# An mLSTM cell feeding a gated MLP: copies and joins of the first cells in another order, and two steps moved in later periods

## The chip, the cores and the metric

The kernel runs on one core of a Trainium2 chip. A core has five engines that run their own queues of instructions in order and wait for each other through semaphores: TensorE (PE, matmuls; its weight loads are shown as PEld), VectorE (DVE), ScalarE (ACT), GpSimd (POOL) and SyncE (SP), which here only issues DMA copies. The metric is the device time of one execution in microseconds, given as the median of several executions.

## The reference, cut to what matters

Two blocks are chained. The first is an mLSTM cell with 4 batch rows, 8 heads, 768 steps and a head size of 40:

```
m_new = max(f + m, i);  f_stab = exp(f + m - m_new);  i_stab = exp(i - m_new)
C = f_stab * C + i_stab * outer(v, k);   n = f_stab * n + i_stab * k
y = sigmoid(o_gate) * (C q) / max(|n . q|, 1)
```

The second takes the 3072 x 320 result x: `h = x @ w_in` (320 x 2048), `g = h * cos(h)`, `out = g @ w_out` (2048 x 320). All is float32.

## The kernel before, in words

The recurrence is worked in 6 chunks of 128 steps. One *cell* n is one chunk of one batch row (8 heads), so there are 24 cells, n = 4 * chunk + row. For a cell the kernel takes the scores k.q (scores, line 443), weighs them with a decay matrix E of 128 x 1024 (weigh, line 453), multiplies by v (values, line 469), divides by the denominator and multiplies by the sigmoid of the output gate (normalize, line 528, giving z), and turns z for the MLP (seam, line 572; seam_out, line 593, copies it to xT). seam also makes the update of the state, pu, which state (line 599) copies or adds. E is a broadcast copy from DRAM (load_E, line 340), from which a per-column value is subtracted (decay_exponents, line 370: VectorE line 372, then GpSimd's select, line 373), and then ScalarE's exp (decay, line 380). The queries and keys are turned by TensorE (turn, line 424; turn_out, line 435, copies them out of PSUM). From cell TURNED = 7 on they are instead loaded in blocks and turned by VectorE (turn_blocks, line 406), and turn_gates (line 414) multiplies the query by its gate and turns the output gates.

The MLP takes a chunk of 4 rows (512 columns) at a time. Up (line 610) multiplies two blocks of 128 rows of w_in with xT (lines 624 and 627, the second for the last 64 rows of w_in, held in w_in_l). h * cos(h) takes four steps a block: near (ScalarE, line 632), rest (VectorE, 635), sin (ScalarE, 640), gate (VectorE, 644). PSUM holds one pair of blocks, so the next Up waits for the gate of the one before. down (line 747) multiplies g with w_out and adds up. From chunk 1 on down_parted (line 686) uses seven products of half width for two of the rows; it needs differences of w_out (differences, line 658) and sums of g (sums, line 675), both made by GpSimd.

The weights come as 64-bit numbers. They are loaded in pieces (weights_in, line 156: two pieces of 512 columns and one for w_in_l; weights_out, line 167), and made into float32 by parts (line 132: two ScalarE steps, lines 138 and 140) and join (line 143: three VectorE steps, lines 144, 146 and 148, and an addition on GpSimd or VectorE, line 149).

The order of the work is written out by hand: no scheduler moves an instruction. first_cells (line 771) works cells 0 to 3 and prepares cell 4, with warm (line 766) putting matmuls without use between. Then both_parts(c, b) (line 907) is a *period*: two Ups of chunk c, with the work of cell 4(c+1)+b between them. The gates of each period stand in VectorE's queue with the joins, the cell's normalization and the turns, so VectorE's order sets when the next Up may start. All copies but four go through SP's queue, in its order; ScalarE loads a table (ACT_TABLE_LOAD) where it goes from one of exp, sigmoid and sin to another.

PSUM tiles come from three pools of rotating buffers: ps_u (2 buffers; its first two tiles are pw and pmu, used by the first cells), ps_a (2) and ps_o (4). psum(n) (line 397) gives the pool of a cell's tiles.

Of the kernel before, what the change touches and what calls it, by code (L numbers as in the profile page):

```python
# [29 lines left out]
def kernel(  # L30
# [22 lines left out]
    B, H, S, D = q.shape  # L53
# [16 lines left out]
    TURNED = 2 * B - 1  # L70
# [269 lines left out]
    def load_E(n):  # L340
        c, b = divmod(n, B)
        E = p4.tile([128, H, C], FP, name="E", tag="E")
        if n not in SPREAD:
            src = M_d[0][ts(b, H)] if c == 0 else M_d[1][ts(b, H), ts(c - 1, C)]
            nc.sync.dma_start(out=E, in_=src.unsqueeze(0).to_broadcast([128, H, C]))
        Es[n] = E
# [225 lines left out]
    def seam(n):  # L572

        pool, tag = psum(n)
        if n < TURNED:

            px = pmu[:, 0:NK + 1] if n < B - 1 else pool.tile([128, NK + 1, C], FP, name="px", tag=tag)
            for i in range(NK + 1):
                nc.tensor.transpose(px[:, i], ys[n][:, ts(i, 128)], ident)
            pxs[n] = px  # L580
        if n < N - B:

            if n < B - 1:
                pu = pw.rearrange("r p t -> r (p t)")[:, 0:HP * D1].rearrange("r (p d) -> r p d", p=HP)
            else:
                pu = pool.tile([128, HP, D1], FP, name="pu", tag=tag)
            for p in range(HP):
                for j in range(2):
                    nc.tensor.matmul(pu[64 * j:64 * j + D, p], kws[n][:, 2 * p + j], vs[n % NB][:, 2 * p + j],  # L589
                                     start=True, stop=True)  # L590
            pus[n] = pu
# [63 lines left out]
    def parted(c):  # L655
        return c > 0
# [114 lines left out]
    def first_cells():  # L771
        nc.vector.memset(nil, 0.0)
        gates_in()
        nc.scalar.copy(out=ident_b, in_=ident)
        load(0, "qk")
        later_gates_in()
        load(1, "qk")
        load(0, "v")
        load_o(0, (0, 1))
        load(2, "qk")  # L780
        load_E(0)
        load_E(1)
        warm(9)
        gates_first()
        later_fills()
        gates_first_out()
        wall_in(0, 0, pmu)
        wall_in(0, 1, psum_o())
        spread(0, 0)
        decay_exponents_half(0, 0)  # L790
        turn(0)
        turn_out(0, False)
        gates_sums()
        spread(0, 1)
        decay_exponents_half(0, 1)
        decay(0)
        weigh_k(0)
        load_E(2)
        load(1, "v")
        load(3, "qk")  # L800
        load_o(0, (2, 3))
        load_E(3)
        load(2, "v")
        load(3, "v")
        pieces.extend(weights_in(0))
        wall_in(1, 0, psum_o())
        wall_in(1, 1, psum_o())
        gates_less_sums()
        spread(1, 0)
        decay_exponents_half(1, 0)  # L810
        scores(0)
        gates_maxima()
        turn(1)
        weigh(0)
        turn_out(1, False)
        sigmoid(0, slice(0, 2))
        spread(1, 1)
        decay_exponents_half(1, 1)
        gates_exponents()
        decay(1)  # L820
        weigh_k(1)
        values(0)
        normalize(0)
        scores(1)
        turn(2)
        turn_out(2, False)
        warm(2)
        seam(0)
        weigh(1)
        seam_out(0)  # L830
        state(0)
        load(B)
        decay_exponents(2)
        decay(2)
        weigh_k(2)
        gates_exp()
        values(1)
        load_E(B)
        outs.append((0, weights_out(0)))
        load_o(1, (0,))  # L840
        load_E(B + 1)
        normalize(1)
        scores(2)
        turn(3)
        sigmoid(0, slice(2, 4))
        seam(1)
        weigh(2)
        decay_exponents(3)
        turn_out(3)
        gates_diagonal()  # L850
        seam_out(1)
        values(2)
        decay(3)
        weigh_k(3)
        state(1)
        normalize(2)
        scores(3)
        pg = gates_turn()
        warm(1)
        seam(2)  # L860
        weigh(3)
        join(*parts(*pieces.pop(0)))
        pieces.extend(weights_in(1))
        load(B + 1)
        outs.extend((p, weights_out(p)) for p in range(1, 3))
        load_o(1, (1, 2, 3))
        seam_out(2)
        second = parts(*pieces.pop(0))
        state(2)
        gates_keep(*pg)  # L870
        values(3)
        normalize(3)
        warm(5)
        seam(3)
        join(*second, nc.vector)
        decay_exponents(B)
        seam_out(3)
        join(*parts(*pieces.pop(0)), nc.vector)
        load_E(B + 2)
        state(3)  # L880

    def cell_after_first():
# [24 lines left out]
    def both_parts(c, b):  # L907

        n = (c + 1) * B + b
        cell = n < N
        begin = c == b == 0
        more = cell and n + 1 < N
        f2 = 2 * b
        up = Up(c, f2, cell_after_first if begin else None)
        if cell:
            scores(n)
            if begin:  # L920
                values_kept(n)

                warm(6, psum_o())
        for e in range(2):
            up.near(e)
        if begin:
            weigh(n)
        for e in range(2):
            up.rest(e)
        if cell and not begin:  # L930
            weigh(n)
        if begin or more and c > 0:
            decay_exponents(n + 1)
        for e in range(2):
            up.sin(e)
            up.gate(e)
        sums(c, f2)
        if n == TURNED:
            turn_gates(n)
        if c == 0 and b == 1:  # L940
            sigmoid(1, slice(1, B))
        if begin:
            sigmoid(1, slice(0, 1))
        if b == B - 1 and c + 2 < NC:
            sigmoid(c + 2)
        h = ()
        if c == 0 and not begin:
            out_join(*out_parts())
        if pieces:
            h = parts(*pieces.pop(0))  # L950
        rest = None
        if b == 0 and c > 0 and parted(c - 1):
            rest = down(c - 1, NF // 2 - 1)
        if begin or more and c > 0:
            decay(n + 1)
        elif more:
            decay_by_bias(n + 1)
        if f2 > 0:
            down(c, f2 - 1)
        elif rest:  # L960
            rest()
        elif c > 0:
            down(c - 1, NF // 2 - 1)
        if cell:
            if n + 2 < N:
                load(n + 2)
            if n < TURNED:
                if not begin:
                    values_kept(n)
                values(n)  # L970
                normalize(n)
            else:
                values_turned(n)
            if h:
                join(*h)
            if TURNED <= n + 2 < N:
                load_G(n + 2)
            if n + 3 < N:
                load_E(n + 3)
            if b == B - 2 and c + 2 < NC:  # L980
                load_o(c + 2)
            if n >= TURNED:
                normalize_turned(n)
            fade(n)
        h = ()
        sin_next()
        if pieces:
            h = parts(*pieces.pop(0))
        up = Up(c, f2 + 1)
        if cell:  # L990
            seam(n)
        for e in range(2):
            up.near(e)
        for e in range(2):
            up.rest(e)
        if cell and n < TURNED:
            seam_out(n)
        if h:
            join(*h)
        if cell:  # L1000
            state(n)
        for e in range(2):
            up.sin(e)
            up.gate(e)
        sums(c, f2 + 1)
        if more:
            weigh_k(n + 1)
        if c == 0 and b == B - 1 or c == 1 and b < B - 1:
            two_differences(c * (2 * b + 2))
        if pieces:  # L1010
            join(*parts(*pieces.pop(0)))
        down(c, f2)
        if pieces:
            join(*parts(*pieces.pop(0)))
        if c == 0:
            if b + 2 < B:
                pieces.extend(weights_in(b + 2))
            h = out_parts()
        if more and n + 1 < TURNED:
            turn(n + 1)  # L1020
            turn_out(n + 1, c > 0)
        elif more:
            turn_blocks(n + 1)
            if n + 1 > TURNED:
                turn_gates(n + 1)
        if c == 0:
            out_join(*h)

    pieces, outs = [], []
    with tc.manual_schedule():  # L1030
# [35 lines left out]
```

## Time and profile before

| What | us |
|---|---|
| Median of 3 executions (lowest, highest) | 537.99 (536.78, 539.98) |
| The profiled execution's own time | 537.05 |
| Its span, first to last instruction | 535.3 |
| TensorE busy | 522.5 |
| VectorE busy | 368.9 |
| ScalarE busy | 260.5 |
| GpSimd busy | 167.8 |
| First Up begins | 35.42 |
| Last matmul ends | 531.8 |

The span is what the engines' instructions take from first to last; the execution's own time is longer by what lies around it. Busy time counts instructions, not queues that wait. Matmul times overlap, so a busy TensorE is not one at its peak. The timeline names a group of like instructions by start, duration, engine, line, operation and tiles; in brackets stands how long the engine was idle before it, and what ended that. The waits list an engine's line, whom it waited for, the total, the number of times and the longest. The chain follows the work that ended last back to what released each step.

In 40 slices of the span, the 16 DMA engines are 90% busy or more in the first eight slices (to 107 us) and less later.

### The profile page before, as it was taken

Reading aid. Unit: us, or ns where it says so; the run is one execution under the profiler, and the core shown is the slowest. Engines: PE = TensorE matmul, PEld = TensorE weight load, DVE = VectorE, ACT = ScalarE, POOL = GpSimd, SP = SyncE. Lnnn points to the kernel's source line nnn. Section 1 sums busy time; section 2 is a strip of 40 time slices with the busy share of each in tenths; the row PEclk is TensorE's granted clock in tenths of the full one; section 3 lists DMA queues with packets and bytes.
Section 4 is the critical chain, followed back from the end, with each engine's and each line's share of the span. In section 5 each row is a group of like instructions: output and inputs, shape, how many; then the busy total and the mean of one; then the engine's idle time right before and its main releaser. Section 6 shows DMA issues by size and latency. Waiting matters only on the chain.

```text
span 535.3 us, 10028 instructions
## 1 busy us (share of the span) xinstructions
PE 522.5 (98%) x3663; PEld 329.9 (62%) x3663; DVE 368.9 (69%) x734; ACT 260.5 (49%) x413; POOL 167.8 (31%) x305
## 2 busy tenths in 40 slices
PE   9888999999999999999999999999999999999997
PEld 6755666655565665566666656656756756656555
DVE  6778778898777687777767777767776765422323
ACT  4868696774633544543436525427335322332312
POOL 7512433525263453223222322422212211212121
PEclk9999999999999999999999999999999999999999
DMA  9999999942265742166735076535075000010001
GB/s 136 216 219 236 218 229 226 206 110 64 83 130 128 159 100 74 62 130 141 154 75 113 13 174 140 140 81 120 7 181 106 11 15 11 8 47 2 0 0 50
DMA packets 134857, 57.76 MB, mean 108 GB/s; under 512 B 70248, under 2 KB 130872, under 8 KB 134808
## 3 DMA queue, kind: packets, MB, share of 16 engines
q1 hardware_dynamic: 134664, 56.93, 47.7%
q8 instruction: 29, 0.48, 0.4%
q0 software_dynamic: 96, 0.18, 0.2%
q14 instruction: 20, 0.16, 0.1%
q10 hardware_dynamic: 48, 0.02, 0.0%
HBM read 50.76 MB, written 6.34 MB: 107 GB/s over the span
## 4 chain that ended last, share of the span: by engine, by line
PE 82%; SPq 5%; DMA 4%; DVE 4%; ACT 2%; issue 1%; POOL 1%; DVEq 0%; POOLq 0%; ACTq 0%
PE po L700 32%; PE pup L624 28%; PE pup L627 9%; PE po L757 3%; PE hp L493 3%; PE ps L450 3%; SPq L329 2%; PE hp L487 2%; DMA bits<-in_moe_w_in_dram 1%; DMA E<-M_d 1%; SPq L129 1%; PE pu L589 1%; DMA qs<-in_q_dram 1%; DVE wt L148 1%; SPq L300 1%
## 5 line engine op out<-in xcount | busy, mean ns | idle before, releaser
L624 PE MATMUL pup<-xT,w_in_sb 128*128 128x512 f32 x384 | 175.1, 598 | 0.7 <-DVE g L644 0.3
L632 ACT ACTIVATE n<-pup 128x512 int32<-128x512 f32 x96 | 52.0, 593 | 212.5 <-PE pup L627 212.5
L635 DVE SCALAR_TENSOR_TENSOR n<-pup,n 128x512 f32<-128x512 f32 x96 | 61.9, 686 | 119.9 <-ACT n L632 119.9
L700 PE MATMUL po<-w_out_sb,g 128*128 128x320 f32 (+1 forms) x480 | 118.6, 396 | 0.0
L624 PEld LDWEIGHTS pup<-xT,w_in_sb 128*128 128x128 f32 x384 | 69.7, 190 | 73.2 <-issue 63.4
L700 PEld LDWEIGHTS po<-w_out_sb,g 128*128 128x128 f32 x480 | 83.5, 190 | 36.7 <-issue 9.1
L683 POOL TENSOR_TENSOR sg<-g 128x128 f32<-128x128 f32 x80 | 36.6, 458 | 193.0 <-DVE g L644 191.6
L640 ACT ACTIVATE n<-n 128x512 f32<-128x512 f32 x96 | 58.9, 630 | 12.4 <-DVE n L635 12.4
L644 DVE SCALAR_TENSOR_TENSOR g<-pup,n 128x512 f32<-128x512 f32 x96 | 61.7, 685 | 2.5 <-ACT n L640 1.2
L627 PE MATMUL pup<-xT,w_in_l 64*128 64x512 f32 x192 | 54.2, 641 | 2.0 <-DVE w_in_l L149 2.0
L373 POOL TENSOR_SCALAR_AFFINE_SELECT E<-E 128x1024 f32<-128x1024 f32 x19 | 20.8, 1094 | 101.5 <-DVE E L372 80.4
L700 PE MATMUL po<-T,sg 128*128 128x160 f32 x240 | 39.4, 300 | 0.0
L757 PE MATMUL po<-w_out_sb,g 128*128 128x320 f32 x128 | 36.6, 439 | 1.7 <-POOL w_out_sb L149 1.7
L627 PEld LDWEIGHTS pup<-xT,w_in_l 64*128 64x128 f32 x192 | 14.4, 184 | 38.5 <-issue 35.6
L700 PEld LDWEIGHTS po<-T,sg 128*128 128x128 f32 x240 | 34.8, 190 | 0.2
L411 DVE STREAM_TRANSPOSE t<-qs 128x512 f32<-128x512 f32 x34 | 34.7, 1098 | 0.0
L450 PEld LDWEIGHTS ps<-t,t 40*128 40x128 f32 (+1 forms) x384 | 25.1, 188 | 9.7 <-issue 9.4
L456 DVE TENSOR_TENSOR E<-ps,E 128x512 f32<-128x512 f32 x48 | 30.7, 681 | 0.4 <-PE ps L450 0.4
L381 ACT ACTIVATE E<-E 128x1024 f32<-128x1024 f32 x21 | 22.2, 1057 | 17.5 <-POOL E L373 16.2
L757 PEld LDWEIGHTS po<-w_out_sb,g 128*128 128x128 f32 x128 | 23.7, 190 | 11.4 <-POOL w_out_sb L149 2.1
L450 PE MATMUL ps<-t,t 40*128 40x128 f32 (+1 forms) x384 | 25.8, 274 | 0.0
L372 DVE TENSOR_TENSOR E<-E,tab 128x1024 f32<-128x1024 f32 x19 | 23.1, 1217 | 3.4 <-DMA E<-M_d 3.4
(152 smaller groups left out, 634.3 us busy)
## 6 DMA issues: line engine op xcount, KB each, us to landing
E<-M_d SPq DMA_DIRECT2D x22, 512.0 KB
bits<-in_moe_w_in_dram SPq DMA_DIRECT2D x40, 128.0 KB
bits<-in_moe_w_out_dram SPq DMA_DIRECT2D x8, 640.0 KB
room<-G_d SPq DMA_DIRECT2D x34, 128.0 KB
ks<-in_k_dram SPq DMA_DIRECT2D x24, 160.0 KB
vs<-in_v_dram SPq DMA_DIRECT2D x24, 160.0 KB
o<-in_o_gate_dram SPq DMA_DIRECT2D x68, 40.0 KB
qs<-in_q_dram SPq DMA_DIRECT2D x34, 80.0 KB
```

The lines of the kernel that those rows point to most:

```text
L411: nc.vector.transpose(out=dst.rearrange("r p (t x) -> r p x t", x=T4), in_=src.rearrange("r p (x d) -> r p x d", x=T4)[:, :, :, 0:32])
L450: nc.tensor.matmul(ps[j][:, p], kT[r, p], qT[r, p], start=True, stop=True)
L456: nc.vector.tensor_tensor(out=w, in0=pss[n][j], in1=w, op=OP.mult)
L624: nc.tensor.matmul(pu, w_in_sb[:, i, ts(block(f2, e), 128)], x(i), start=(i == 0), stop=False)
L627: nc.tensor.matmul(pu, w_in_l[r, f2], x(NK, r), start=False, stop=True)
L632: nc.scalar.activation(out=self.n[e], in_=self.pu[e], func=AF.Copy, bias=0.25)
L635: nc.vector.scalar_tensor_tensor(out=self.n[e].bitcast(FP), in0=self.pu[e], scalar=0.25, in1=self.n[e], op0=OP.add, op1=OP.subtract)
L640: nc.scalar.activation(out=r, in_=r, func=AF.Sin, scale=TWO_PI_DOWN)
L644: nc.vector.scalar_tensor_tensor(out=g, in0=self.pu[e], scalar=TWO_PI, in1=self.n[e].bitcast(FP), op0=OP.mult, op1=OP.mult)
L683: nc.gpsimd.tensor_tensor(out=S[:, i], in0=x, in1=y, op=op)
L700: nc.tensor.matmul(out, g, w, start=(f2 == 0 and first), stop=end, skip_group_check=True)
L757: nc.tensor.matmul(po[c][b], gs[c, f][:, ts(b, C)], w_out_sb[:, f], start=(f == 0), stop=(f == NF - 1))
```

## The change

Nothing is computed otherwise; the order of steps changes in two places, and one tile's pool and the number of warming matmuls.

In first_cells: v of cell 2 and E of cell 3 are loaded ahead of the output gates of rows 2 and 3; E of cell 4 ahead of that cell's q and k, and its v behind the first piece of w_out. On VectorE the copy of cell 3's turned keys goes ahead of that cell's exponents. The sigmoid of rows 2 and 3 goes behind cell 3's exp and the first weight piece's parts. values(3) goes ahead of cell 2's normalization and seam. The exponents of cell 4 go behind the join of w_in_l, and the state copies of cells 2 and 3 to the end. There are 14 warming matmuls in place of 6 in this stretch. Cell 2's pu comes from the pool ps_a and not from the tile pw.

In both_parts: cell 7's turn_blocks, which stood at the end of the period of cell 6, stands behind that cell's fade in the period's middle. In later periods turn_gates stands behind the join of w_out (where chunk 0 has one), and in the last period of chunk 0 the first two differences stand behind that join.

```diff
--- before.py
+++ after.py
@@ -580,7 +580,7 @@
             pxs[n] = px
         if n < N - B:
 
-            if n < B - 1:
+            if n < B - 2:
                 pu = pw.rearrange("r p t -> r (p t)")[:, 0:HP * D1].rearrange("r (p d) -> r p d", p=HP)
             else:
                 pu = pool.tile([128, HP, D1], FP, name="pu", tag=tag)
@@ -798,9 +798,9 @@
         load_E(2)
         load(1, "v")
         load(3, "qk")
+        load(2, "v")
+        load_E(3)
         load_o(0, (2, 3))
-        load_E(3)
-        load(2, "v")
         load(3, "v")
         pieces.extend(weights_in(0))
         wall_in(1, 0, psum_o())
@@ -829,54 +829,56 @@
         weigh(1)
         seam_out(0)
         state(0)
-        load(B)
+        load_E(B)
+        load(B, "qk")
         decay_exponents(2)
         decay(2)
         weigh_k(2)
         gates_exp()
         values(1)
-        load_E(B)
         outs.append((0, weights_out(0)))
+        load(B, "v")
         load_o(1, (0,))
         load_E(B + 1)
         normalize(1)
         scores(2)
         turn(3)
-        sigmoid(0, slice(2, 4))
         seam(1)
         weigh(2)
+        turn_out(3)
+        seam_out(1)
         decay_exponents(3)
-        turn_out(3)
         gates_diagonal()
-        seam_out(1)
         values(2)
         decay(3)
         weigh_k(3)
         state(1)
-        normalize(2)
         scores(3)
+        weigh(3)
         pg = gates_turn()
-        warm(1)
-        seam(2)
-        weigh(3)
+        warm(5)
+        values(3)
         join(*parts(*pieces.pop(0)))
+        sigmoid(0, slice(2, 4))
+        gates_keep(*pg)
         pieces.extend(weights_in(1))
         load(B + 1)
         outs.extend((p, weights_out(p)) for p in range(1, 3))
         load_o(1, (1, 2, 3))
+        normalize(2)
+        warm(5)
+        seam(2)
         seam_out(2)
         second = parts(*pieces.pop(0))
-        state(2)
-        gates_keep(*pg)
-        values(3)
         normalize(3)
-        warm(5)
+        warm(4)
         seam(3)
         join(*second, nc.vector)
-        decay_exponents(B)
         seam_out(3)
         join(*parts(*pieces.pop(0)), nc.vector)
+        decay_exponents(B)
         load_E(B + 2)
+        state(2)
         state(3)
 
     def cell_after_first():
@@ -982,6 +984,8 @@
             if n >= TURNED:
                 normalize_turned(n)
             fade(n)
+            if n + 1 == TURNED:
+                turn_blocks(n + 1)
         h = ()
         sin_next()
         if pieces:
@@ -1005,8 +1009,8 @@
         sums(c, f2 + 1)
         if more:
             weigh_k(n + 1)
-        if c == 0 and b == B - 1 or c == 1 and b < B - 1:
-            two_differences(c * (2 * b + 2))
+        if c == 1 and b < B - 1:
+            two_differences(2 * b + 2)
         if pieces:
             join(*parts(*pieces.pop(0)))
         down(c, f2)
@@ -1019,12 +1023,14 @@
         if more and n + 1 < TURNED:
             turn(n + 1)
             turn_out(n + 1, c > 0)
-        elif more:
+        elif more and n + 1 > TURNED:
             turn_blocks(n + 1)
-            if n + 1 > TURNED:
-                turn_gates(n + 1)
         if c == 0:
             out_join(*h)
+            if b == B - 1:
+                two_differences(0)
+        if more and n + 1 > TURNED:
+            turn_gates(n + 1)
 
     pieces, outs = [], []
     with tc.manual_schedule():
```

## The prediction

> **What bounds the kernel now.** I read the page's busy shares and its chain first, then the waits of TensorE, then the timeline around each of those waits.
>
> ```profile
> PE 522.5 (98%) x3663; PEld 329.9 (62%) x3663; DVE 368.9 (69%) x734; ACT 260.5 (49%) x413; POOL 167.8 (31%) x305
> ...
> PE 82%; SPq 5%; DMA 4%; DVE 4%; ACT 2%; issue 1%; POOL 1%; DVEq 0%; POOLq 0%; ACTq 0%
> ```
>
> TensorE is busy 98% of the span. The chain in order of time runs on other engines until about 117 us and from 134 us on it is unbroken TensorE work to 531.8. So a part of this change pays only if it shortens what TensorE waits for before 134 us. Its waits over the whole span:
>
> ```profile
> PE pup L627 <- DVE w_in_l L149: 2.0, 1, 2.0
> PE ph L475 <- DMA vs<-in_v_dram: 1.9, 1, 1.9
> PE po L757 <- POOL w_out_sb L149: 1.7, 2, 1.3
> PE pw L769 <- ACT st L603: 1.6, 1, 1.6
> ```
>
> The first, second and fourth lie in the first cells, the third is two waits in chunk 0's last period and chunk 1's first. The timeline (start, duration, engine, line) there:
>
> ```profile
> 29.58 1.98 PE L475 MATMUL ph<-vs,E 128*128 128x41 f32 x16
> 33.19 1.24 PE L769 MATMUL pw<-nil 128*128 128x512 bf16 x5 [1.64 <-ACT st L603]
> 35.42 1.96 PE L624 MATMUL pup<-xT,w_in_sb 128*128 128x512 f32 x4 [0.22 <-ACT xT L597]
> 37.94 1.23 DVE L372 TENSOR_TENSOR E<-E,tab 128x1024 f32<-128x1024 f32 x1 [2.37 <-DMA E<-M_d]
> 39.73 0.79 ACT L138 ACTIVATE wt<-bits 128x640 f32<-128x640 f32 x1 [0.81 <-DMA bits<-in_moe_w_out_dram]
> 41.10 1.04 ACT L381 ACTIVATE E<-E 128x1024 f32<-128x1024 f32 x1
> 41.95 1.13 PE L627 MATMUL pup<-xT,w_in_l 64*128 64x512 f32 x4 [1.99 <-DVE w_in_l L149]
> 43.11 1.08 ACT L632 ACTIVATE n<-pup 128x512 int32<-128x512 f32 x2 [0.97 <-PE pup L627]
> 45.99 1.23 ACT L640 ACTIVATE n<-n 128x512 f32<-128x512 f32 x2 [0.50 <-DVE n L635]
> 104.87 1.29 DVE L644 SCALAR_TENSOR_TENSOR g<-pup,n 128x512 f32<-128x512 f32 x2
> 107.23 2.03 DVE L411 STREAM_TRANSPOSE t<-qs 128x512 f32<-128x512 f32 x2
> 112.71 4.57 PE L757 MATMUL po<-w_out_sb,g 128*128 128x320 f32 x16 [1.27 <-POOL w_out_sb L149]
> 129.23 0.69 DVE L418 TENSOR_TENSOR room<-t,room 128x512 f32<-128x512 f32 x1
> 134.34 4.57 PE L757 MATMUL po<-w_out_sb,g 128*128 128x320 f32 x16 [0.43 <-POOL w_out_sb L149]
> ```
>
> The reader sees that the last rows of w_in come late because VectorE, ahead of their join, stands 2.37 us before cell 4's exponents for their broadcast; and that ScalarE works without a gap from 45.99 to the second n at 55.03, whose gate ends the wait at 59.9. So ScalarE's start of sin sets TensorE's time there. From 59.9 to 107 TensorE is busy in all of the 47 us.
>
> **What the Trainium skill says.** "DMA: Bandwidth & Descriptors", section on queues, rings and completion order: each DMA engine takes its ring in order. The landings in the trace agree: in SP's order, with the next one 0.5 to 2.9 us behind, and 16 engines 0.9 to 1.1 busy from 10 to 56 us. So moving a copy ahead delays exactly those it passes. "ScalarE: Activation LUTs", section on what a table load costs: about 1283 ns plus a drain of some 1380. The trace shows the 1.28 and no drain (load ends 51.42, exp starts 51.44); I use 1.28. "SBUF — State Buffer", section on its two sides: VectorE and GpSimd lock a shared port pair. The trace agrees: the 128x256 shift at line 146 took 1.07 us beside GpSimd's select at 39.24, and 0.29 at 60.75.
>
> **The change, part by part.**
>
> *First cells, copies.* By last landing, 160 KB copies come 0.5 to 1.0 us apart, a broadcast some 2 to 2.9. Before: o of rows 2 and 3 at 20.27 and 20.74, E3 23.64, v2 24.28. v2 now takes the first place: 20.3; E3 follows, one small copy ahead of before: 22.7. values(2) no longer waits 1.87. The weights stay at 27.46 (first piece), 31.33, 32.40. Before, q4, k4, v4, E4, w_out piece 0 landed at 33.30, 34.24, 35.03, 37.84, 39.65. Now E4, q4, k4, w_out, v4: about 34.8, 35.7, 36.5, 38.7, 39.6. v4 is first read near 44.
>
> *First cells, up to the first Up.* Unchanged to weigh(2), which ends at 22.61. Then the copy of k (0.68) to 23.23; E3's exponents 1.23, to 24.4; select 1.09, to 25.5; exp at 25.6, with no table load ahead of it, to 26.7 (before 27.95); weigh(3) 1.29, to 28.0 (before 29.27). ScalarE: two state copies 0.58, to 27.2; wt and wm of the first piece wait for 27.46 and take 1.27, to 28.8; table load 1.28 and sigmoid 0.74, to 30.8. This is the new cost: y of cell 2 needs that sigmoid, so z of cell 2 ends at 32.0 (1.1 from y to z), where before it ended at 28.03; z of cell 3 follows 1.62 later, at 33.6 (before 33.21). TensorE: values(3) 28.4 to 30.3, five warming matmuls (1.24) to 31.5, seam(2) 32.05 to 33.1, four more to 34.1, seam(3) transposes to 34.4. The eight added warming matmuls cost nothing while z is late; without that cover they would cost 0.21 each. ScalarE: seam_out(2) to 33.25, wt and wm of the second piece 1.25, to 34.45, seam_out(3) 0.48, to 34.95. First Up at 35.1 against 35.42: only 0.3 won. pu of cell 2 now lies in the pool of the pt tiles, so cell 4's transposes of k wait for state(2) on ScalarE: done at 36.3, wanted at 37.9; nothing.
>
> *First cells, after the first Up.* The join of w_in_l now stands ahead of E4's exponents. VectorE: z 33.6, second piece 2.4, to 36.2, third piece about 1.5, to 37.8; wanted by TensorE 4.54 us after Up's start (39.96 - 35.42 before), 39.6. The wait of 1.99 goes; line 627 runs 39.6 to 40.8. What is late next is ScalarE: its copies of cell 4's k end at 38.6, w_out lands at 38.7, wt and wm 1.47, to 40.2; then the exp table that used to be loaded already, 1.28, to 41.5; exp 1.06, to 42.55. n can start only behind it: 42.5 against 43.11. Then 1.08 and sin's table 1.28: sin at 44.9 against 45.99 (the 0.50 it waited for VectorE goes too: weigh(4) ends 43.9, the first rest 44.6). So 1.09 won of about 2.3. Everything on ScalarE from there is unbroken and its inputs have landed (E5 43.15, w_in 45.15), so TensorE's period at 59.9 begins 1.05 sooner.
>
> *Cell 7's transposes.* Two of 1.10, pipelined 1.87 to the next start. They move from 107.23 to 100.56, behind a join and ahead of the first rest at 101.29, where VectorE had idled 0.66. All behind them on VectorE is 1.14 later, so the first gate ends at 106.70, not 105.56, and Up waits until about 106.8, not 105.89: 0.9 lost. In the next period the join of w_out no longer stands behind them: VectorE ends it at 110.3, GpSimd at 112.0; TensorE, 0.9 late, wants it at 112.3 (112.71 - 1.27 + 0.9). The wait of 1.27 goes, net 0.4 won. turn_gates(7) has its product with the query at about 116, and TensorE reads it near 117.
>
> *w_out join ahead of turn_gates, differences behind it.* VectorE ends the join 1.66 sooner, GpSimd's 1.54 end at 132.7; wait 0.43 gone. turn_gates ends at 132.8, read at 138.4. The eight differences, 0.53 each, end at 137.0; T is read at 145.6.
>
> Sum: 1.05 + 0.4 + 0.43 = 1.9 us. The profiled span of 535.3 becomes 533.4, that execution's 537.05 becomes 535.15. The median of 537.99 lies 0.94 above it, so I give 537.99 - 1.9 = **536.1**.
>
> Unknowns, with both ends. How w_out lands between E4 and k4 isn't shown: at 38.6 or sooner (ScalarE is the limit then, +0.1 won) to 39.65 as before (sin at 45.85, 0.9 less); I take 38.7. VectorE's delay by the transposes: 0 if they find room, 2.0 if they collide with GpSimd's join at 100.72; between 1.27 won and 0.5 lost, and I take 0.4.
>
> **The rivals.** (a) All ends are kind: gate not late, so the transposes cost nothing and the 1.27 comes whole: 1.15 + 1.27 + 0.43 = 2.85, 535.1. For it: VectorE idles 1.25 before 96.1 and could run ahead. Against: VectorE takes its queue in order, and the transposes stand behind that stretch. (b) The first cells win nothing, since the sigmoid and its table only change places: w_out lands at 39.65 as before, 0.15 + 0.83 = 1.0, 537.0. For it: both table loads remain. Against: one copy fewer lies ahead of w_out. (c) Slower: w_out is late, because E4's broadcast drags. Each us of landing past 39.8 puts sin, and TensorE at 59.9, a us later; at 40.6 the other 0.83 is eaten, at 43.4 the kernel is 2.8 slower, 540.8. For it: before, one copy's slowest engine ended 2.1 us behind its fastest. Against: ring order. That the table load isn't in the queue, or that the joins don't move, is excluded by the order of instructions.
>
> **How the numbers follow.** Half a per cent, 2.7 us, is about what a measurement here can tell from no change: 535.3 to 540.7 is same. Forecast 0.52 (its own range 535.0 to 537.2; 0.05 of it under 535.3), (a) 0.28, (b) 0.14, (c) 0.06. Faster: 0.28 + 0.05 = 0.33; same: 0.47 + 0.14 = 0.61; slower 0.06. The range reaches 1 us beyond (a), since a median of three moved by that much among 536.78, 537.99 and 539.98, and on the other side beyond (b) by the same 1.2: 534.0 to 538.2.
>
> **What would show it.** Right: no TensorE wait on w_in_l nor on v; an exp table load right behind line 140 near 40.2, and n right behind exp near 42.5; a TensorE wait of about 0.9 on the gate near 105, and no waits on w_out_sb. Wrong: n waiting for TensorE (then more is won), w_out landing past 39.8, TensorE waiting on the gate for 2 us or not at all, or a first Up away from 35.1.

## The result, and the profile after

Side by side, the changed kernel took 536.87 us (median of 20 executions, 535.45 to 543.71) and the kernel before 539.47 us (20 executions): a ratio of 0.9958, 95% interval 0.9942 to 0.9973. Two later comparisons of the same two kernels gave 0.9970 (0.9947 to 0.9994) and 0.9988 (0.9969 to 1.0007). Over all of them the mean went from 538.52 us (213 executions) to 537.29 us (53, without the disturbed one below): 1.2 us less, with a standard error of 0.24. These means pool executions of several comparisons. The three ratios, each from one comparison, give 0.9970 when weighted by their intervals: 1.6 us less, with an interval from 1.0 to 2.2. The forecast was 1.9 us less.

The first execution that was profiled stood still for 5 us at 123 us because of one late copy, so another is shown: its own time is 536.17 us, its span 534.5, and as in the one shown of before TensorE has its full clock throughout. The page's busy shares and its chain:

```profile
PE 524.6 (98%) x3671; PEld 330.5 (62%) x3671; DVE 368.2 (69%) x734; ACT 260.8 (49%) x413; POOL 169.0 (32%) x305
...
PE 81%; SPq 7%; DMA 6%; ACT 3%; DVE 2%; issue 1%; POOL 0%; POOLq 0%; ACTq 0%
```

TensorE's part of the chain has not grown, though its first cells run without the old waits; DMA and SP's queue hold 13% now and held 9% before. TensorE's waits:

```profile
PE pt L431 <- issue: 1.6, 1, 1.6
PE pw L769 <- DVE nil L772: 1.1, 1, 1.1
PE pup L624 <- DVE g L644: 1.0, 1, 1.0
PE pup L624 <- POOL w_in_sb L149: 0.7, 1, 0.7
PE pw L769 <- ACT st L603: 0.4, 1, 0.4
```

The four waits shown of before (on w_in_l, on v, on w_out_sb, on st) are gone or down to 0.4. New are 1.6 us ahead of a transpose of keys and 0.7 us on GpSimd's join of w_in; that on the first gate grew from 0.3 to 1.0. The timeline at the places that were shown of before, and at the start of the second period (57.85, before 59.90):

```profile
28.16 1.88 PE L475 MATMUL ph<-vs,E 128*128 128x41 f32 x16
34.47 1.95 PE L624 MATMUL pup<-xT,w_in_sb 128*128 128x512 f32 x4 [0.23 <-ACT xT L597]
37.86 0.81 ACT L138 ACTIVATE wt<-bits 128x640 f32<-128x640 f32 x1
38.95 1.13 PE L627 MATMUL pup<-xT,w_in_l 64*128 64x512 f32 x4
39.38 1.28 ACT L381 ACT_TABLE_LOAD   x1
40.67 1.06 ACT L381 ACTIVATE E<-E 128x1024 f32<-128x1024 f32 x1
41.64 1.07 ACT L632 ACTIVATE n<-pup 128x512 int32<-128x512 f32 x2
44.02 1.15 ACT L640 ACTIVATE n<-n 128x512 f32<-128x512 f32 x2
57.85 2.38 PE L624 MATMUL pup<-xT,w_in_sb 128*128 128x512 f32 x5
100.60 2.08 DVE L411 STREAM_TRANSPOSE t<-qs 128x512 f32<-128x512 f32 x2
105.93 1.29 DVE L644 SCALAR_TENSOR_TENSOR g<-pup,n 128x512 f32<-128x512 f32 x2
106.77 3.67 PE L624 MATMUL pup<-xT,w_in_sb 128*128 128x512 f32 x8 [0.72 <-POOL w_in_sb L149]
112.33 4.57 PE L757 MATMUL po<-w_out_sb,g 128*128 128x320 f32 x16
133.45 4.57 PE L757 MATMUL po<-w_out_sb,g 128*128 128x320 f32 x16
```

The first cells work better than forecast: the second period begins 2.05 us sooner, not 1.05. At 106.77, though, TensorE is 0.88 us later than before (105.89). Between the two, 2.9 us have gone.

**Where they went.** ScalarE's timeline of the kernel before, at the place where it begins to decode the next piece of w_in:

```profile
69.47 0.77 ACT L138 ACTIVATE wt<-bits 128x640 f32<-128x640 f32 x1
70.14 0.79 ACT L140 ACTIVATE wm<-bits 128x640 int32<-128x640 uint32 x1
70.91 0.68 ACT L138 ACTIVATE wt<-bits 128x512 f32<-128x512 f32 x1
```

and of the changed kernel:

```profile
67.42 0.77 ACT L138 ACTIVATE wt<-bits 128x640 f32<-128x640 f32 x1
68.09 0.80 ACT L140 ACTIVATE wm<-bits 128x640 int32<-128x640 uint32 x1
70.91 0.68 ACT L138 ACTIVATE wt<-bits 128x512 f32<-128x512 f32 x1 [2.02 <-DMA bits<-in_moe_w_in_dram]
```

ScalarE comes 2.05 us sooner and waits 2.02 us, until the piece has landed: at 70.80, where before it had landed at 70.81. But not all of the piece was asked for sooner. SP's queue sends it as four copies. The first goes out 1.02 us sooner (62.19, before 63.21), but the third takes 1.49 us to issue, where before it took 0.42, and so the fourth goes out when it did before. That fourth copy before:

```profile
65.36 0.42 SPq L129 DMA_DIRECT2D bits<-in_moe_w_in_dram  x1
```

and in the changed kernel:

```profile
65.35 0.42 SPq L129 DMA_DIRECT2D bits<-in_moe_w_in_dram  x1
```

The DMA engines are busy throughout in both kernels until 69 us; in the last 2 us ahead of the landing they are less than half busy in the changed one. The windows (length, busy time of PE, PEld, DVE, ACT, POOL, then TensorE's clock, the share of the 16 DMA engines and GB/s), before:

```profile
60.00:69.00 9.00, 9.00 (x41) 5.24 (x42) 7.25 (x13) 6.43 (x10) 2.96 (x3) 1.00 1.23 248
69.00:71.00 2.00, 2.00 (x15) 1.71 (x14) 0.70 (x2) 2.00 (x4) 0.00 (x0) 1.00 0.94 221
```

and after:

```profile
60.00:69.00 9.00, 9.00 (x52) 6.07 (x50) 6.04 (x10) 6.29 (x9) 1.98 (x2) 1.00 1.21 228
69.00:71.00 2.00, 2.00 (x17) 1.76 (x17) 1.86 (x4) 0.09 (x1) 0.75 (x1) 1.00 0.45 129
```

So the end of the piece comes late although the engines have room again by then, and its last copy left no sooner. Why SP took longer over the third copy is not shown. Nor is 70.8 a fixed time: in the other execution of the changed kernel (the first experiment below) the four copies went out from 61.75 to 63.84 and had landed at 70.00.

From 70.91 on ScalarE keeps the same times in both kernels, to 0.02 us, for 12 us. The chain of the changed kernel in order of time (start, duration, what), with the steps between left out:

```profile
65.35 5.45 DMA bits<-in_moe_w_in_dram
...
70.91 0.68 ACT wt L138
...
78.57 0.49 ACT n L632
...
81.19 0.70 DVE wt L148
...
82.05 1.28 POOL w_in_sb L149
83.34 3.67 PE pup L624 x8
```

Before, that Up began at 83.33. The copy of 70.8 thus sets TensorE's time at 83.3 in this execution, and of the 2.05 us nothing is left. On TensorE it shows as a wait that the profile puts down to nobody:

```profile
80.40 0.60 PE L431 MATMUL pt<-ident,qs 128*128 128x128 f32 x4
82.57 0.63 PE L431 MATMUL pt<-ident,ks 128*128 128x128 f32 x4 [1.57 <-issue]
```

What remains are the 0.88 us lost at 106 and what is won behind it (1.27 and 0.50): the last matmul ends at 530.9 instead of 531.8, in an execution at full clock.

### The profile page after: what moved, and what is told of

Read it like the earlier page. It is cut to its first block, busy times and chain, and to the rows that moved or that the text cites. A ratio compares the mean times of both kernels' runs of the same rounds, so it can differ in the third digit from the quotient of the medians.

```text
span 542.0 us, 10044 instructions
## 1 busy us (share of the span) xinstructions
PE 527.8 (97%) x3671; PEld 332.4 (61%) x3671; DVE 367.5 (68%) x734; ACT 260.3 (48%) x413; POOL 168.1 (31%) x305
## 4 chain that ended last, share of the span: by engine, by line
PE 77%; SPq 8%; DMA 8%; ACT 5%; issue 1%; DVE 1%; ACTq 0%
PE po L700 31%; PE pup L624 26%; PE pup L627 8%; DMA bits<-in_moe_w_out_dram 4%; SPq L329 3%; PE hp L493 3%; DMA bits<-in_moe_w_in_dram 3%; PE ps L450 3%; PE po L757 2%; PE hp L487 2%; SPq L129 1%; PE pu L589 1%; DMA E<-M_d 1%; ACT wt L138 1%; SPq L345 1%
## 5 line engine op out<-in xcount | busy, mean ns | idle before, releaser
L700 PEld LDWEIGHTS po<-w_out_sb,g 128*128 128x128 f32 x480 | 83.5, 190 | 36.7 <-issue 9.1
L757 PE MATMUL po<-w_out_sb,g 128*128 128x320 f32 x128 | 39.3, 464 | 0.0
L700 PEld LDWEIGHTS po<-T,sg 128*128 128x128 f32 x240 | 34.8, 190 | 0.2
L757 PEld LDWEIGHTS po<-w_out_sb,g 128*128 128x128 f32 x128 | 25.2, 202 | 10.7 <-issue 2.0
```

What stands on the lines that cost most here:

```text
L700: nc.tensor.matmul(out, g, w, start=(f2 == 0 and first), stop=end, skip_group_check=True)
L757: nc.tensor.matmul(po[c][b], gs[c, f][:, ts(b, C)], w_out_sb[:, f], start=(f == 0), stop=(f == NF - 1))
```

## The experiments

From the second period on the traces repeat to about 0.1 us, but for the stretch above and for one more place: between 117 and 123 us VectorE waits for ScalarE ahead of a join of w_out, for 0.16 us in the kernel before but for 1.87, 2.75 and 5.75 in three of the fourteen traces, and in these TensorE waits behind it (1.10 us in the 22.35 below; 5 us in the execution that stood still). So they give what each kernel does there, whatever its first cells did (us; from one start to the next):

| Kernel | second period starts | to the Up at 105.89 | to the down at 112.71 | to the down at 134.34 | to the last matmul's end |
|---|---|---|---|---|---|
| before | 59.90 | 45.99 | 6.82 | 21.63 | 397.46 |
| changed, shown above | 57.85 | 48.92 | 5.56 | 21.12 | 397.46 |
| changed, another execution | 60.12 | 46.67 | 5.55 | 21.13 | 397.45 |
| first cells alone | 61.73 | 45.83 | 6.82 | 21.64 | 397.45 |
| cell 7's turn alone | 63.82 | 46.75 | 5.55 | 21.86 | 397.46 |
| join ahead of turn_gates alone | 61.64 | 45.91 | 6.82 | 21.13 | 397.45 |
| changed, turn ahead of normalize | 62.46 | 46.02 | 5.55 | 21.13 | 397.45 |
| the same, another execution | 57.99 | 48.74 | 5.52 | 21.13 | 397.46 |
| first cells of before, the rest as there | 59.46 | 46.82 | 5.55 | 22.35 | 397.46 |

Where the second period starts at 59.9 or later, the stretch to the next column is its own length; the three that start sooner (57.85, 57.99, 59.46) are 2.3, 2.7 and 0.8 longer than their likes. The last column is constant to 0.01 us. Read from the rows without such waits, the part behind the first cells is worth, against before, 1.09 us in the changed kernel (0.68 lost, 1.27 and 0.50 won), 0.28 for the turn alone, 0.58 for the join alone, 1.74 with the turn ahead of normalize. The traces differ most in where the second period starts, by several us.

**The changed kernel again,** without an edit.

> The changed kernel once more, for an undisturbed profile. Sum theory (first cells 1.05 as predicted, transposes 0.4, join 0.43): ratio 0.9965, second period's first Up at 58.8. Rival (first cells win about 2, because the first w_out piece lands near 37.3 and not 38.7): ratio near 0.995, that Up near 57.9. Both: no TensorE wait on w_in_l, v or w_out_sb, and a wait of 0.6 to 1.0 on a gate or on w_in_sb near 105.

Ratio 0.9970 (0.9947 to 0.9994), between the two and not telling them apart. Its second period starts at 60.12, at neither 58.8 nor 57.9: in its trace TensorE stood at half its clock from 47.8 to 51.2, which lengthened the second Up of the first period from 3.70 to 5.40 us.

**The first cells alone.** The kernel before, with the edits to first_cells and to seam, and both_parts as it was.

```diff
 # both_parts as before; of the change only
-            if n < B - 1:
+            if n < B - 2:
 # and the new order of first_cells
```

> Only the first cells in the new order; all periods as before. As predicted: 1.05 us, ratio 0.998, n of the first Up at 42.5, the second period's first Up at 58.8. Rival: about 2 us, ratio 0.9963, n near 41.7, Up near 57.9. Both keep the waits of about 1.3 and 0.4 on w_out_sb, since the periods are as before.

Ratio 1.0006 (0.9982 to 1.0030): no gain, and the predicted 0.998 lies just outside the interval and the rival's 0.9963 well outside. The waits that they remove are gone from its trace, too. What remains is the old waits behind, and two that have grown: on cell 0's E (before 0.2) and on the first gate (before 0.3):

```profile
PE po L757 <- POOL w_out_sb L149: 1.7, 2, 1.3
PE ph L475 <- DVE E L456: 1.1, 1, 1.1
PE pup L624 <- DVE g L644: 1.0, 1, 1.0
```

**Cell 7's turn alone.**

```diff
             fade(n)
+            if n + 1 == TURNED:
+                turn_blocks(n + 1)
 ...
-        elif more:
+        elif more and n + 1 > TURNED:
             turn_blocks(n + 1)
-            if n + 1 > TURNED:
-                turn_gates(n + 1)
+            turn_gates(n + 1)
```

> Only cell 7's transposes moved into the middle of cell 6's period. As predicted: gate 1.14 later, Up 0.9 later near 106.8, the wait of 1.27 on w_out_sb gone, net 0.4: ratio 0.9993. Rival (the transposes find room): no new wait, net 1.27: ratio 0.9976. Rival (they collide with GpSimd's join and cost 2): net loss of 0.5, ratio 1.001. First cells as before, wait of 0.43 near 134 kept.

Ratio 0.9999 (0.9983 to 1.0015), where the trace's 0.28 us would give 0.9995.

```profile
PE pup L624 <- POOL w_in_sb L149: 0.7, 1, 0.7
PE po L757 <- POOL w_out_sb L149: 0.7, 1, 0.7
```

The wait of 1.27 is exchanged for one of 0.68 at 106, and the one at 134 grows from 0.43 to 0.66.

**The join ahead of turn_gates alone, with the differences behind it.**

```diff
-        if c == 0 and b == B - 1 or c == 1 and b < B - 1:
-            two_differences(c * (2 * b + 2))
+        if c == 1 and b < B - 1:
+            two_differences(2 * b + 2)
 ...
-            if n + 1 > TURNED:
-                turn_gates(n + 1)
         if c == 0:
             out_join(*h)
+            if b == B - 1:
+                two_differences(0)
+        if more and n + 1 > TURNED:
+            turn_gates(n + 1)
```

> Only the join of w_out ahead of turn_gates and the first two differences behind it. As predicted: the wait of 0.43 near 134 goes and nothing else moves, ratio 0.9992. Rival (differences are late for their product near 145): a new TensorE wait on T of up to 2 us, ratio up to 1.003.

Ratio 0.9977 (0.9959 to 0.9995); the trace's 0.58 us, 0.9989, lies inside. Of the two waits on w_out_sb one is left, of 1.3. Each part by itself is thus small, and first cells alone gave nothing. The clock records suggested a reason: in this trace TensorE stood at half clock for 10.2 us from 27.6, in that of the turn alone for 17.1 us from 24.5. An execution's mean clock was 0.99 or less in 78 of 193 executions of the kernel before and, over all three comparisons, in 2 of the 54 of the changed one whose clock is on record (one more than in the means above), which has fewer gaps and more warming matmuls. So the gain might be one of the clock. Two experiments ask that.

**Few warming matmuls in the changed kernel.**

```diff
         pg = gates_turn()
-        warm(5)
+        warm(1)
 ...
-        warm(5)
         seam(2)
 ...
-        warm(4)
         seam(3)
```

> The changed kernel with the earlier number of warming matmuls in the first cells: 1 where it has 5, 5 and 4, all else as changed. Sum theory (the prediction's): those thirteen matmuls are covered by the wait for z, so nothing moves: 537.1 as the changed kernel has, ratio to the kernel before 0.997, the first Up of the same execution at its place within 0.2 us. Clock theory (a gap in TensorE's work lets the granted clock fall to half for the next stretch of 3.4 us or several, and the change pays mostly because it leaves fewer gaps): the gaps return, about a third of the executions show a mean clock of 0.99 or less, as in the kernel before, against none of 32 of the changed kernel, and the mean is 1 to 1.5 us longer than the changed kernel's, ratio 0.9995 to 1.0005.

The clock did what the clock theory says: 12 of 22 executions at 0.99 or less. The time did not: 536.78 us, ratio 0.9984 (0.9966 to 1.0003), a mean of 537.21 where the changed kernel, in another comparison, had 537.11. In its trace the stretch from 30 to 40 us runs at half clock, and TensorE is still not full:

```profile
30.00:40.00 10.00, 9.26 (x58) 6.91 (x58) 8.64 (x24) 8.01 (x18) 1.27 (x1) 0.52 1.09 212
```

**More warming matmuls in the kernel before.**

```diff
+        warm(6, psum_o())
         values(2)
 ...
+        warm(6, psum_o())
         warm(5)
         seam(3)
 ...
+            if between:
+                warm(6, psum_o())
             for e, pu in enumerate(self.pu):
```

> The kernel before with six warming matmuls of 0.21 us in each of its three waits of the first cells (ahead of values of cell 2, ahead of the five there are before the seam of cell 3, and ahead of the last rows of the first Up), nothing else changed. Sum theory: the work on the chain is the same or 0 to 1 us longer where a wait is shorter than 1.3 us, so ratio 1.000 to 1.002. Clock theory: fewer executions at a mean clock of 0.99 or less (2 in 20 instead of 7 in 20), so 1 us shorter in the mean, ratio 0.997 to 0.999.

No execution of 22 at 0.99 or less, and 1.0029 (1.0011 to 1.0046): slower. As it was put, the clock theory falls: in both experiments the warming matmuls moved the clock, and the time didn't follow.

That doesn't make the clock harmless. Of the 193 executions of the kernel before, the 78 at 0.99 or less average 539.98 us, the other 115 average 537.45. Of the changed kernel's 54 all but 2 are of the second kind, and these average 537.08. So at like clock it is only some 0.4 us faster, and more of its 1.2 us comes from the executions at low clock that it hardly has. With few warming matmuls 12 executions at 0.99 or less average 538.34 and the other 10 average 535.86: at like clock quicker than the changed kernel, and more often at low clock. A gain and a loss of about one size would fit both experiments. That is a reading of averages, for a mean clock does not tell where the slow stretch lay. Nor is all of the 1.0029 the matmuls' own: in its profiled execution 1.65 of the 2.9 us over the profile of before lie between 114 and 137 us, behind the wait of 2.75 us named above, where none was added.

**Cell 7's transposes ahead of cell 6's normalization.**

```diff
+                if n + 1 == TURNED:
+                    turn_blocks(n + 1)
                 normalize(n)
 ...
-            if n + 1 == TURNED:
-                turn_blocks(n + 1)
         h = ()
```

> The changed kernel with the two transposes of cell 7 ahead of the normalization of cell 6 instead of behind it: they fall into the 1.25 us in which VectorE waits for TensorE near 95 us. Expected: z of cell 6 ends near 99.9 instead of 99.2 (TensorE reads it at 100.6), the first rest starts near 101.4 instead of 102.56, and TensorE's wait of 0.68 us at 106 on GpSimd's join of w_in is gone: 0.7 us shorter than the changed kernel, ratio 0.9955 to 0.9965. Rival: the transposes and GpSimd's join of w_out at 94.4 hold each other up, z is late for TensorE and the gain is nothing: ratio 0.997.

The trace shows the wait at 106 gone and 45.99 kept (46.02 in the table), as expected. The time doesn't: 1.0000 (0.9977 to 1.0022).

**The sigmoid of cells 2 and 3 back behind turn(3).**

```diff
         turn(3)
+        sigmoid(0, slice(2, 4))
         seam(1)
 ...
         join(*parts(*pieces.pop(0)))
-        sigmoid(0, slice(2, 4))
         gates_keep(*pg)
```

> The changed kernel with the sigmoid of cells 2 and 3 back behind the turn of cell 3, ahead of cell 3's exponential, so that the two table loads stand on the other side of it again. Sum theory: cell 3's exponential waits for a table load, 28.0 instead of 26.7, the second table load at 40.2 is not needed (the exp table stays in), and cell 4's exponential and sin are ScalarE's 1.28 us sooner; z of cells 2 and 3 is up to 1.5 us sooner, but values of cell 3 start 1.3 later. I expect the first Up 0 to 0.5 later and sin 0.5 to 1.0 sooner, in all 0.5 us shorter than the changed kernel, ratio 0.995 to 0.997. Rival: the move is what the first cells gain by; then 1 us longer, ratio 0.999.

Slower than the kernel before: 1.0025 (1.0004 to 1.0046). Its profiled execution, one of the two quickest of 16, doesn't show it: with the clock as in the trace of the first cells alone up to 50 us, the first Up begins at 37.29 against 37.60. But 13 of the 16 executions have a mean clock of 0.99 or less. By these times the move of the sigmoid is worth having. There are 14 warming matmuls here too, so their number alone doesn't set the clock; why so much of it goes is not shown.

**Four kernels at once.** By then there were two readings: that the first cells win on average (A), or that they don't (B). The first is the changed kernel's part behind the first cells, with the turn ahead of normalize, on the first cells of before:

> The first cells of the kernel before, with all that the change does behind them, cell 7's transposes ahead of cell 6's normalization as in the experiment that tried that. From the start of the second period on the traces repeat to 0.01 us, so this part is known: 1.75 us shorter than before (the wait of 1.27 and that of 0.43 gone, no new one at 106), whatever the first cells do. Both theories: ratio 0.9967, with 0.002 either way for where the first cells end in each execution; second period starting as the kernel before's does, 61.2 on average.

Ratio 0.9960 (0.9943 to 0.9978), with 0.9967 expected. The changed kernel beside it:

> The changed kernel once more, beside the other three. Theory A (the changed first cells are 1 to 2 us shorter, as the traces with TensorE at full clock show): 1.1 from the part behind the first cells and 1.5 from them, ratio 0.995. Theory B (averaged over executions the changed first cells win nothing, since the waits they removed were the room in which a late or halved TensorE clock cost nothing): 1.1 alone, ratio 0.998.

Ratio 0.9988 (0.9969 to 1.0007): B's 0.998, not A's 0.995. This is the execution shown above, with the wait of 2.02 us on the piece of w_in, which neither reading had named. The turn ahead of normalize once more:

> The changed kernel with cell 7's transposes ahead of cell 6's normalization, once more: 1.75 from the part behind the first cells. Theory A: with 1.5 more from the first cells, ratio 0.994, and 1.5 us shorter than the same part behind the first cells of before. Theory B: ratio 0.9967, equal to that kernel within 0.5 us. That the first measurement of this kernel, 1.000, is a property of it and not chance would show as 1.000 again.

Ratio 0.9989 (0.9967 to 1.0011). It is not faster than the changed kernel and, against both readings, 0.0029 or 1.6 us slower than the same part on the old first cells, though the intervals overlap. The first measurement, 1.0000, had said so as well. In its trace the same copy is late, by 0.8 us more:

```profile
71.74 0.67 ACT L138 ACTIVATE wt<-bits 128x512 f32<-128x512 f32 x1 [2.70 <-DMA bits<-in_moe_w_in_dram]
```

And with few warming matmuls:

> The changed kernel with cell 7's transposes ahead of cell 6's normalization and with 1 warming matmul where the change has 5, 5 and 4. Theory A: as without the second edit, ratio 0.994 to 0.995. Theory B: the fewer matmuls give a little room back in which a slow TensorE costs nothing, but more stretches at half clock come with it: ratio 0.9955 to 0.9975, mean clock 0.994 or less in most executions.

Ratio 0.9969 (0.9951 to 0.9986), 13 of 22 executions at 0.99 or less: as B has it.

In the trace of the old first cells with the new rest, the second period starts at 59.46, only 0.44 us ahead of the profile of before, and the same limit is met already:

```profile
71.25 0.67 ACT L138 ACTIVATE wt<-bits 128x512 f32<-128x512 f32 x1 [0.76 <-DMA bits<-in_moe_w_in_dram]
```

So in the four traces whose second period starts before 59.9 (three with the changed first cells, of which the disturbed one waits 1.62 us there, and this one) the gain is cut off by a landing of the same piece, at 70.4 to 71.6 us; in the nine of the other kernels and executions that start later, and in before's, there is no wait on it. No kernel that asks for that piece earlier was tried.

## Why the prediction was right, and where it was not

The predicted time, 536.1 us, lies 0.8 under the measured median and well inside the range, and "same" was the likeliest class. That it came so near is in part luck. The forecast subtracted 1.9 from 537.99; in the comparison the kernel before took 539.47, and the changed one 2.6 less. The sum behind it was right in two terms of three and wrong in the largest.

- *What the first cells win: 1.05 forecast.* The chain was right, step by step: v of cell 2 landed at 20.2 (20.3) with no wait for it, E of cell 3 at 21.9 (22.7), cell 3's exp ran from 25.49 (25.6 forecast), the waits on v and on w_in_l went, and an exp table load stands behind line 140 with n right behind exp. The sizes were cautious: z of cell 2 ended at 31.7 (32.0), the first Up began at 34.47 (35.1), w_out's first piece landed at 37.8 (38.7), sin began at 44.02 (44.9), the second period at 57.85 (58.8). What was mis-sized is the landings: E of cell 4 came at 33.3, its q and k at 35.1 and 35.9, against estimates of 34.8, 35.7 and 36.5, and with them w_out, which sets ScalarE's table load, n and sin.
- *That this gain reaches the end.* This step failed: "From 59.9 to 107 TensorE is busy in all of the 47 us". It is true and doesn't carry the conclusion. A busy TensorE says that nothing is late for it at its present pace; how much sooner the others could be must be asked of each. ScalarE at 70.91 had no wait, but also no room: the copy it read had landed 0.1 us before. Of 2.05 us nothing was left at 83.3. The Up at 59.90 already showed what to look for. The prediction has it wait for a gate; in the chain of before a join of w_in ends last there, and such a join needs such a piece:

```profile
58.61 1.29 POOL w_in_sb L149
59.90 3.67 PE pup L624 x8
```

- *The transposes of cell 7: 0.4 net.* Right to 0.2: the first rest began 1.2 us later (102.53 against 101.29), TensorE waited at 106 and the wait of 1.27 went. The wait came from GpSimd's join of w_in (ended 106.77), behind VectorE's part of it, and not from the gate, whose first half ended 0.15 us before; 0.68 lost, not 0.9, so 0.59 won where the period starts late, and 0.39 in the execution shown.
- *The join ahead of turn_gates: 0.43.* It measured 0.50; the wait at 134 is gone.
- *That the eight added warming matmuls cost nothing while z is late.* Held at full clock: the second five end at 31.1 and z of cell 2 comes 0.4 later, the four end at 33.5, when z of cell 3 has just come (33.3). So they cost 0.2 us at most there. Over executions the kernel with 1 in place of the 5, 5 and 4 is no faster and no slower, 0.9984 beside 0.9970 and 0.9988; at like clock it looks quicker (535.86 against 537.08), so whether they are free on average is open.
- *Rival (b), the first cells win nothing, 537.0,* had 0.14. The first cells alone (1.0006) and the execution shown agree with it, and the rest gives 1.09 us by the traces. Its size is not decided: the pooled mean fell by 1.2, the weighted ratios say 1.0 to 2.2 us, and the forecast's 1.9 lies inside, too. Its cause was another one, a late w_out, which came sooner than forecast.
- *Not foreseen at all* was TensorE's clock. The executions of one kernel differ by 3 us and more, the longer ones mostly at a lower mean clock, and in all traces but one the stretches at half that lie under TensorE's work fall into the first 60 us. With that the first cells' gain may fail in another way. With the old order, 17.1 us at half clock in the turn alone put the second period 3.9 us behind 59.90, and 10.2 us in the join alone, with full clock first granted at 7.2 instead of 3.8, put it 1.7 behind: 0.17 to 0.23 us for each. With the new order 6.8 us put it 3.9 (first cells alone) and 4.6 (turn ahead of normalize) behind 57.85: 0.6 to 0.7. The shortest stretches say the same: with 3.4 us at half clock the old first cells with the new rest started 0.4 ahead of 59.90, the changed kernel's other execution 2.3 behind 57.85. This would follow if the waits that were removed had been room for a slow TensorE. But these stretches lie at other places, and no experiment set the clock, so it is likely and not shown.

Open is why the turn ahead of normalize gains nothing on the new first cells (1.0000 and 0.9989) when it gains its full 1.74 us on the old ones (0.9960, so 2.2 us), and with few warming matmuls seems to gain something on the new ones, too (0.9969 beside 0.9984); why SP's third copy was slow to go out; and why the sigmoid's old place brings so many stretches at half clock. On these numbers the old first cells with the new rest are at least as good as the changed kernel: the intervals, 0.9943 to 0.9978 and 0.9969 to 1.0007 in the same comparison, overlap slightly.

## What to carry to other kernels

A stall that is removed early is worth only as much as the next limit lets through: before a gain is carried to the end, look at each engine in the stretch behind it for inputs that land just as they are read, for a wait of zero is not slack. Then ask when the late input was sent for: work that moves ahead on one engine does not by itself move the queue that feeds it. Where executions differ by more than the change, split the time at points that every trace repeats; here the stretch behind 134 us agreed to 0.01 us and those ahead of it, where no copy was late, to about 0.1, and they gave each part's worth, which 20 executions could not. A gap may be absorbing a varying clock or a late copy; closing it then pays less on average than in the one execution that was profiled. The runs here fit that and don't prove it.

## What was not expected of the hardware

TensorE's granted clock is halved for stretches of 3.4 us or multiples of it (3.4, 6.8, 10.2 and 17.1 us in the traces), at other places in each execution, and the first full clock came at 3.8 to 7.2 us. The Trainium skill, "TensorE: Matmul & The Clock Gate", Part 1 on the clock gate, has a window of some 3.4 us that runs freely, and a start that varies with it; the traces agree, and in each of them the stretches at half begin a whole number of such windows behind the first full clock (47.84 - 6.88 us is 12 times 3.41). Its rule in the same part, that TensorE should have no idle gaps over some 3.4 us, is too mild for this kernel: the execution with the stretch at half clock from 47.8 has no wait of TensorE over 1.1 us, while three waits of 1.6 to 2.0 us in the profile of before were followed by none. The share of executions at a mean clock of 0.99 or less was 40% in the kernel before, 4% in the changed one with eight warming matmuls more, none with eighteen more in the old waits, but 13 of 16 with the eight more and the sigmoid at its old place. Within the kernel before such executions were 2.5 us longer; between kernels the share did not tell which was faster.
